# Eight more chunks solved in blocks of 32, early parts dealt later, and three inputs loaded in runs of eight steps

## The chip, the cores and the metric

The kernel runs on one core of a Trainium2 chip. The metric is the time of one execution in microseconds on the device; the median of three runs is given beside the lowest and the highest. The profile is taken from one more execution. In it, PE is the matrix engine and PEld its weight loads, DVE the vector engine, ACT the scalar engine, POOL the GpSimd engine, and SP an engine that here only issues DMAs.

## The reference

Two stages. The first is a recurrence over 768 steps for 4 batches x 8 heads with a state of 40 x 40 each; the second is a feed-forward network with a squared ReLU on its output.

```python
for t in range(S):                       # S = 768, D = 40
    y[:, :, t] = einsum('bhd,bhde->bhe', rt, state)
    Sa = einsum('bhde,bhe->bhd', state, at)
    state = state * wt[:, :, None, :] - einsum('bhd,bhe->bhde', Sa, bt) + einsum('bhd,bhe->bhde', vt, kt)
x = y.transpose(0, 2, 1, 3).reshape(B * S, H * D)     # 3072 x 320
h = maximum(x @ w_in, 0)                 # 320 x 2048
out = (h * h) @ w_out                    # 2048 x 320
```

The inputs of the recurrence are float32, laid out as batch, head, step, d. The weights w_in and w_out come as float64; the kernel reads their words and makes float32 of them.

## The kernel before

**Chunks.** The recurrence is done in 24 chunks of 128 steps, six for each batch; `order` (line 136) goes over the batches first, so chunks 0 to 3 are the first ones of the four batches. Within a chunk the steps depend on each other through a triangular system; its inverse is a matrix per head. A chunk has four parts:

- `early` (line 341) needs only w, a and b. It turns them so that d lies on the partitions (`turn`, line 311: four transposes on PE into one PSUM tile), makes running products of w in both directions with scans on DVE (lines 351, 352), reciprocals (355, 356), scales b and a (359, 360), and multiplies them to the triangular matrix N, which ACT copies out of PSUM (367 to 372). The pieces of N and the scaled rows are stored to DRAM (`kept_e`, `kept_q`, `kept_d`, `kept_m`, `kept_n`), because they are made several chunks ahead.
- `solve` (417, `solving` 420) inverts the triangular blocks on POOL, one column per step and two instructions per column (443, 445). It takes a whole unit of one, two or four chunks at once: `take` (406) reads their blocks from DRAM into `half_n`, and line 448 writes the inverse to `kept_t`. Units below `FINE` (line 299) are solved in blocks of `Q` = 32 steps, which is 31 columns; the others in blocks of `HC` = 64, which is 63 columns, with rows up to twice as long.
- `rest` (502) loads k, r, v, turns them, makes the masked products A and RV, and fetches the inverse (`inverses`, 452). For a unit of blocks of 64 the inverse comes straight into the tile `T`. For blocks of 32 it comes into `blocks`, and two blocks are joined into one of 64: a transpose on DVE (477), copies on ACT (479), 16 products on PE (487), a copy (489), 16 more products (494), a copy (496). `soon` (500) says whether the fetch is issued early in `rest`.
- `chain` (569) is the sequential part: eleven steps from PE to ACT or DVE and back, which use the state, T and N, and end in the tokens of the chunk.

**FFN.** `ffn` (663) works on groups of three chunks: eight steps with the first weight matrix, ReLU on ACT (679), squares on DVE (661), then twelve steps with the second. A group is 20 steps, all groups 160. It can start when three chunks are done and the first ten of 26 weight pieces are made. `rounding` (249) makes these pieces from the raw words, five DVE and two ACT instructions each; the raw words are staged in `w_out` and in `hidden`, whose last four tiles hold the small tiles of `spare` (337).

**Order.** After a prologue written out by hand (750 to 792), iteration i runs `chain(i)`, a share of FFN steps, one or two `prepare` (an `early`, with the loads of the next one), `rest(i + 1)` and some weight pieces. `weave` (707) deals their generator steps over twelve slots and emits the instructions in that order, which is the order of each engine's queue; what a generator has left after the twelve slots is run at the end, one generator after the other. `rest` gets nine steps in slots 2 to 11. `ahead` (796) says which early parts iteration i makes, `by_then` (802) how many FFN steps are done after it, `pieces_in` (806) how many weight pieces. After each iteration every unit whose chunks are all made is solved. One unit, number 4, is solved in two halves with an iteration between them (`AHEAD`, 810).

**Loads.** `fetch` (139) puts a chunk of an input into a ring tile `[128 steps, 8 heads, 64]`, of which 40 are data and 24 are a pad that a memset fills once. A load so has 1024 pieces of 40 words, 160 B each. All loads and most stores are issued by SP, in one queue.

Line 87 is the helper through which nearly all products go, line 314 the transposes of `turn`, line 108 all stores.

Of the kernel before, what the change touches and what calls it, by code (L numbers as in the profile page):

```python
# [12 lines left out]
Act = mybir.ActivationFunctionType  # L13
# [4 lines left out]
def kernel(  # L18
# [22 lines left out]
    nc = tc.nc  # L41
    ctx.enter_context(tc.manual_schedule())
    B, H, S, D = r.shape
# [45 lines left out]
    def single(name, shape):  # L89
        return const.tile(shape, FP32, tag=name, name=name)  # L90
# [25 lines left out]
    class Ring:  # L116
        def __init__(self, name, n, shape, fill, pads):
            self.tiles = [single(f"{name}{i}", shape) for i in range(n)]
            self.at = -1
            for t_ in self.tiles:  # L120
                nc.gpsimd.memset(pads(t_), fill)
# [4 lines left out]

    pads = lambda t_: t_[:, :, D:]
    rings = {}
    for nm, n, fill in (("w", 2, 1.0), ("ab", 4, 0.0)):
        rings[nm] = Ring(f"in_{nm}", n, [128, H, DP], fill, pads)  # L130

    def more_rings():
        for nm in ("k", "b", "r", "v"):
            rings[nm] = Ring(f"in_{nm}", 1 if nm == "r" else 2, [128, H, DP], 0.0, pads)

    order = [(bb, c) for c in range(NCH) for bb in range(B)]
    loaded, early_loaded = {}, {}

    def fetch(ring, src, i):
        bb, c = order[i]  # L140
        t_ = rings[ring].next()
        nc.sync.dma_start(out=t_[:, :, :D], in_=src[bb, :, c * C:(c + 1) * C, :].rearrange("h t d -> t h d"))
        return t_
# [27 lines left out]

    which = single("which", [128, 2])
    nc.gpsimd.memset(which, 0.0)
    for n in range(4):
        nc.gpsimd.memset(which[n * 32:(n + 1) * 32, n % 2:n % 2 + 1], 1.0)

# [118 lines left out]

    sizes = [1, 1] + [2] * 4 + [4] * ((len(order) - 12) // 4) + [2]
    units = [(sum(sizes[:u]), n) for u, n in enumerate(sizes)]

    FINE = 4
    SMALL = units[FINE][0]  # L300
# [10 lines left out]
    def turn(x_):  # L311
        p_ = psum(ps_w)
        for q in range(NP):
            nc.tensor.transpose(p_[:, q * 128:(q + 1) * 128], pair(x_, q), ident)  # L314
        return quads(p_)

    def products(l_, r_):
# [18 lines left out]

    def spare(name, i):
        at = NF * GB * C - (("mv", "turned", "joins").index(name) * 2 + i % 2 + 1) * H * Q
        return free_words[:, at:at + H * Q].rearrange("p (h t) -> p h t", h=H)

    def early(i, g=None):
# [5 lines left out]
        up, down, aT = (dec[:, n] for n in (UP, DOWN, A_))  # L347
        wT = turn(x_["w"])
        yield
# [3 lines left out]
        yield  # L353
        bT_, aT_ = turn(x_["b"]), turn(x_["a"])
        nc.vector.reciprocal(down[:, :, MID + 1:C + 1], up[:, :, MID + 1:C + 1])  # L355
# [30 lines left out]
        if g is None:  # L386
            store(kept_n[i], t_[:HC, :, HC:], 1)
        else:
            g["dec"], g["N"] = dec, new("N21", [HC, H, HC], 2)
            nc.scalar.copy(g["N"], t_[:HC, :, HC:])  # L390
            g["joins"] = spare("joins", i)
            for half in range(2):
                nc.scalar.copy(g["joins"][half * HC:half * HC + Q], joins(half))
# [8 lines left out]


    EARLIER = Q * HC

    def take(u, queues, words=slice(None)):
        first, nb = units[u]
        if u < FINE:
            kept = kept_q[first:first + nb].rearrange("b h f k s t -> (b h f k) (s t)")
        else:  # L410
            kept = kept_d[u].rearrange("b h f w -> (b h f) w")
        cols = classes(u)
        rows = 128 // cols
        for col in range(cols):
            queues[col % len(queues)].dma_start(out=part_of(u)[col * rows:(col + 1) * rows, words], in_=kept[:, words])  # L415

    def solve(u, between={}):
        run(solving(u, between))

    def solving(u, between={}, stop=None):  # L420

        first, nb = units[u]
        fine = u < FINE
        size = Q if fine else HC
        cols = classes(u)
        rows = 128 // cols
        part = part_of(u)
        words = size // cols * size
        at = u * Q * Q // 2 if fine else 0
        ts = solved[:, at:at + words]  # L430
        nc.gpsimd.memset(ts, 0.0)
        for col in range(cols):
            nc.gpsimd.memset(ts[col * rows:(col + 1) * rows, col::size + cols], -1.0)
        t3 = ts.rearrange("p (j t) -> p j t", t=size)
        for s in range(size - 1):
            if s in between:
                between[s]()
            if s == stop:
                yield
            n, m_ = s // cols + 1, size - 1 - s  # L440
            at = s * size + s + 1 if s < Q else Q * HC + (s - Q) * (Q + 1) + 1
            p_ = new("half_p", [128, 528], 1)[:, :n * m_].rearrange("p (j t) -> p j t", j=n)
            nc.gpsimd.tensor_tensor(p_, part[:, at:at + m_].unsqueeze(1).to_broadcast([128, n, m_]),  # L443
                                    t3[:, :n, s:s + 1].to_broadcast([128, n, m_]), Alu.mult)
            nc.gpsimd.tensor_tensor(t3[:, :n, s + 1:], t3[:, :n, s + 1:], p_, Alu.subtract)  # L445
        to = kept_t[u]
        to = to.rearrange("n b h f k j t -> (n b h f k) (j t)") if fine else to.rearrange("n b h f j t -> (n b h f) (j t)")
        nc.gpsimd.dma_start(out=to, in_=ts)
# [3 lines left out]
    def inverses(i, g, queue=nc.sync):  # L452
# [13 lines left out]
        if "N" not in g:  # L466
            g["N"] = new("N21", [HC, H, HC], 2)
            queue.dma_start(out=g["N"], in_=kept_n[i])
            if u < FINE:
                g["joins"] = spare("joins", i)  # L470
                for half in range(2):
                    queue.dma_start(out=g["joins"][half * HC:half * HC + Q], in_=kept_m[i][half])
        if u >= FINE:
            return
        yield
        upper_ = spare("turned", i)
        nc.vector.transpose(upper_.rearrange("p h t -> p (h t)"), blocks.rearrange("p h t -> p (h t)"))
        for n in range(2):
            nc.scalar.activation(T[:, :, n * Q:(n + 1) * Q], blocks, Act.Copy, scale=which[:, n:n + 1])
        yield  # L480
        small = lambda: psum(ps_w)[:, :H * Q].rearrange("p (h t) -> p h t", h=H)
        p_ = small()
        mv = spare("mv", i)
        ends_ = [(slice(half * HC, half * HC + Q), slice(half * HC + Q, (half + 1) * HC)) for half in range(2)]
        for h in range(H):
# [16 lines left out]
    def rest(i, g):  # L502
# [19 lines left out]
        while "v" not in x_:  # L522
            line.pop(0)[1]()
        nc.scalar.copy(rT, turn(x_["r"]))  # L524
        vT = turned("kvT", 1)
# [137 lines left out]
    def ffn():  # L663
        for gi in range(len(order) // GB):
# [3 lines left out]
            hid = []  # L668
            for f in range(0, NF, 2):
                square(hid[-2:])  # L670
                ps = [psum(ps_f if gi < len(order) // GB - 1 else ps_w)[:, :GB * C] for _ in range(2)]
                for e, p_ in enumerate(ps):
# [12 lines left out]
            for n in range(GB):  # L685
                bb, c = order[gi * GB + n]
                p_ = psum(ps_f if gi < len(order) // GB - 1 else ps_w)[:, :DM]
                for f in range(NF):
                    mm(p_, hid[f][:, n * C:(n + 1) * C], w_out[:, f], f == 0)
                    if f % PART == PART - 1 and f < NF - 1:  # L690
                        yield True
# [11 lines left out]
    def run(gen):  # L703
        for _ in gen:
            tick()
# [89 lines left out]
    TOTAL = 12  # L795
    ahead = {0: (4, 5), 1: (6, 7), 2: (8, 9), 3: (10,), 4: (11,), 5: (12, 13)}
    ahead.update({i: (i + 8,) for i in range(6, 9)})
    ahead[9] = (17, 18)
    ahead.update({i: (i + 9,) for i in range(10, len(order) - 9)})

    PER, LAG = NF // 2 + 4 * GB, 3
    by_then = [0] * B + [5]
    for i in range(B + 1, len(order)):
        by_then.append(min(by_then[-1] + 7, PER * (i + 1) // GB - PER - LAG if i > 2 * B else PER * i))
    share = {i: (n - (by_then[i - 1] if i else 0), 4 if i == B else 0) for i, n in enumerate(by_then)}
    pieces_in = {0: (4, TOTAL), 1: (6, TOTAL), 2: (6, TOTAL), 3: (7, TOTAL), B: (4, 4)}
    done = set(range(B))
    unit = unit_of[B]

    AHEAD, under_way = (FINE,), []  # L810
    for i in range(len(order)):
# [19 lines left out]
        while unit < len(units) and all(m_ in done for m_ in range(len(order)) if unit_of[m_] == unit):  # L831
            flush()
            if under_way:

                take(unit, own, slice(0, EARLIER))
                run(under_way.pop())
                take(unit, own, slice(EARLIER, Q * (HC + Q)))
            else:
                take(unit, own)
            if unit in AHEAD:  # L840
                under_way.append(solving(unit, stop=Q + 1))
                next(under_way[0])
            else:
                solve(unit)
            unit += 1
# [32 lines left out]
```

## Time and profile before

| | |
|---|---|
| median of three runs | 1046.84 us (1044.67 to 1049.31) |
| profiled execution, its own time | 1047.3 us |
| its span, first to last instruction | 1045.6 us |
| mean granted clock of PE | 0.915 |
| PE busy | 927.4 us, 89% of the span |
| PEld busy | 672.1 us, 64% |
| POOL busy | 670.6 us, 64% |
| DVE busy | 496.8 us, 48% |
| ACT busy | 273.0 us, 26% |
| DMA packets | 260360, of these 243724 under 512 B |
| DMA moved | 106.92 MB, 102 GB/s on average |

Busy time is the union of an engine's instructions; a granted clock below 1 says that PE ran at half rate for a part of the time. The start of line 583 marks the first step of each chunk's `chain`: 29.3, 105.4, 154.9, 204.9, 241.0 and 288.9 us for chunks 0 to 5, 479.6 for chunk 10, 645.5 for chunk 14 and 957.1 for chunk 23. The first FFN step's ReLU (679) starts at 252.8 us. POOL writes an inverse back (448) at 49.0, 76.3, 107.9 and 148.0 us for the four units in blocks of 32, at 251.4 and 338.8 for two chunks each in blocks of 64, at 475.1, 609.8 and 747.9 for four chunks each, and at 844.2 for the last two.

### The profile page before, as it was taken

Reading aid. Unit: us, or ns where it says so; the run is one execution under the profiler, and the core shown is the slowest. Engines: PE = TensorE matmul, PEld = TensorE weight load, DVE = VectorE, ACT = ScalarE, POOL = GpSimd, SP = SyncE. Lnnn points to the kernel's source line nnn. Section 1 sums busy time; section 2 is a strip of 40 time slices with the busy share of each in tenths; the row PEclk is TensorE's granted clock in tenths of the full one; section 3 lists DMA queues with packets and bytes.
Section 4 is the critical chain, followed back from the end, with each engine's and each line's share of the span. In section 5 each row is a group of like instructions: output and inputs, shape, how many; then the busy total and the mean of one; then the engine's idle time right before and its main releaser. Section 6 shows DMA issues by size and latency. Waiting matters only on the chain.

```text
span 1045.6 us, 19803 instructions
## 1 busy us (share of the span) xinstructions
PE 927.4 (89%) x7824; PEld 672.1 (64%) x7824; DVE 496.8 (48%) x940; ACT 273.0 (26%) x627; POOL 670.6 (64%) x1128
## 2 busy tenths in 40 slices
PE   6364665688999999997999999999999999999998
PEld 5253455576667766775677766775677567756656
DVE  5556685796554465453744545534432432222120
ACT  3132332334332133122232132113212311232020
POOL 4778454897898599995999949999668820000000
PEclk8656676667999999998999999999999999999999
DMA  8987989688184938198564596064425432520000
GB/s 108 154 145 146 178 196 179 163 158 147 43 137 92 193 55 136 24 164 194 61 113 90 87 183 119 21 118 59 115 50 98 66 72 49 98 30 7 23 0 19
DMA packets 260360, 106.92 MB, mean 102 GB/s; under 512 B 243724, under 2 KB 249356, under 8 KB 258604
## 3 DMA queue, kind: packets, MB, share of 16 engines
q1 hardware_dynamic: 255740, 86.65, 47.8%
q0 software_dynamic: 3440, 18.88, 7.8%
q8 instruction: 62, 1.02, 0.4%
q10 hardware_dynamic: 1088, 0.13, 0.1%
q14 instruction: 30, 0.25, 0.1%
HBM read 72.47 MB, written 31.19 MB: 99 GB/s over the span
## 4 chain that ended last, share of the span: by engine, by line
PE 52%; POOL 28%; DMA 10%; issue 5%; DVE 2%; ACT 2%; SPq 1%; POOLq 0%; DVEq 0%; ACTq 0%
PE ps_f L87 26%; POOL half_t L445 14%; POOL half_p L443 13%; PE ps_w L87 11%; PE ps_c L87 10%; DMA half_n<-kept_d 3%; PE ps_w L314 2%; DMA kept_t<-half_t 1%; DMA half_n<-kept_q 1%; DMA in_w<-in_w_dram 1%; DMA T<-kept_t 1%; DMA w_out<-in_moe_w_in_dram 1%; PE ps_w L542 1%; DMA kept_m<-N 1%; POOL half_n L415 1%
## 5 line engine op out<-in xcount | busy, mean ns | idle before, releaser
L443 POOL TENSOR_TENSOR half_p<-half_n,half_t 128x70 f32<-128x70 f32 (+52 forms) x502 | 298.9, 595 | 90.2 <-DMA half_n<-kept_d 39.8
L445 POOL TENSOR_TENSOR half_t<-half_t,half_p 128x70 f32<-128x70 f32 (+52 forms) x502 | 322.4, 642 | 39.3
L87 PE MATMUL ps_f<-w_out,hid 128*128 128x320 f32 x672 | 198.6, 440 | 0.0
L87 PE MATMUL ps_f<-tokens,w_in 128*128 128x384 f32 x448 | 162.3, 506 | 0.0
L661 DVE TENSOR_TENSOR hid<-hid 128x384 f32<-128x384 f32 x128 | 94.4, 752 | 139.4 <-ACT hid L679 139.0
L87 PEld LDWEIGHTS ps_f<-w_out,hid 128*128 128x128 f32 x672 | 121.6, 190 | 44.9 <-issue 2.1
L87 PEld LDWEIGHTS ps_f<-tokens,w_in 128*128 128x128 f32 x448 | 82.1, 193 | 77.2 <-issue 33.8
L679 ACT ACTIVATE hid<-ps_f 128x384 f32<-128x384 f32 x112 | 54.9, 490 | 201.1 <-PE ps_f L87 201.1
L330 DVE TENSOR_TENSOR A<-ps_w,upper 128x512 f32<-128x512 f32 x48 | 30.9, 686 | 108.0 <-PE ps_w L87 108.0
L87 PE MATMUL ps_w<-decay,bT 40*128 40x128 f32 x352 | 31.7, 330 | 33.2 <-DVE decay L360 29.5
L514 DVE TENSOR_TENSOR kvT<-ps_w,dec 128x512 f32<-128x512 f32 x24 | 16.5, 687 | 88.7 <-DMA dec<-kept_e 46.6
L87 PE MATMUL ps_f<-tokens,w_third 64*128 64x384 f32 x224 | 55.4, 540 | 0.0
L87 PEld LDWEIGHTS ps_w<-decay,bT 40*128 40x128 f32 x352 | 26.9, 229 | 41.8 <-DVE decay L360 26.7
L87 PE MATMUL ps_c<-xr,T 64*64 64x40 f32 x768 | 39.1, 242 | 13.7 <-ACT xr L592 6.7
L351 DVE TENSOR_TENSOR_SCAN decay<-ps_w,ones 128x64 f32<-128x64 f32 x88 | 23.8, 270 | 54.2 <-PE ps_w L314 54.1
L87 PEld LDWEIGHTS ps_c<-xr,T 64*64 64x64 f32 x768 | 32.5, 148 | 25.1 <-ACT xr L592 13.1
L330 DVE TENSOR_TENSOR RX<-ps_w,upper 128x512 f32<-128x512 f32 x48 | 30.8, 683 | 26.2 <-PE ps_w L87 25.9
L330 DVE TENSOR_TENSOR RV<-ps_w,upper 128x512 f32<-128x512 f32 x48 | 30.9, 686 | 18.1 <-PE ps_w L87 17.9
L355 DVE RECIPROCAL decay<-decay 128x256 f32<-128x256 f32 x22 | 38.3, 1739 | 0.0
L356 DVE RECIPROCAL decay<-decay 128x256 f32<-128x256 f32 x22 | 37.3, 1694 | 0.0
L87 PE MATMUL ps_w<-rT,xnT 40*128 40x128 f32 x384 | 34.2, 293 | 2.4 <-ACT rT L524 2.4
L524 ACT COPY rT<-ps_w 128x512 f32<-128x512 f32 x24 | 14.0, 585 | 82.5 <-PE ps_w L314 82.5
(139 smaller groups left out, 1391.0 us busy)
## 6 DMA issues: line engine op xcount, KB each, us to landing
kept_e<-decay SPq DMA_DIRECT2D x22, 633.8 KB
dec<-kept_e SPq DMA_DIRECT2D x22, 633.8 KB
hid<-in_moe_w_out_dram SPq DMA_DIRECT2D x16, 320.0 KB
half_n<-kept_d POOLq DMA_DIRECT2D x6, 768.0 KB, 11.4
in_w<-in_w_dram SPq DMA_DIRECT2D x24, 160.0 KB
in_ab<-in_b_dram SPq DMA_DIRECT2D x24, 160.0 KB
in_ab<-in_a_dram SPq DMA_DIRECT2D x24, 160.0 KB
in_k<-in_k_dram SPq DMA_DIRECT2D x24, 160.0 KB
```

The source lines that it names most:

```text
L87: nc.tensor.matmul(o, l_, r_, start=start, stop=True, skip_group_check=True)
L314: nc.tensor.transpose(p_[:, q * 128:(q + 1) * 128], pair(x_, q), ident)
L330: nc.vector.tensor_tensor(t_, p_, over4(upper), Alu.mult)
L351: nc.vector.tensor_tensor_scan(up[:, q, MID + 1:C + 1], wT[:, q, MID:], ones, 1.0, Alu.mult, Alu.mult)
L355: nc.vector.reciprocal(down[:, :, MID + 1:C + 1], up[:, :, MID + 1:C + 1])
L356: nc.vector.reciprocal(up[:, :, :MID], down[:, :, :MID])
L443: nc.gpsimd.tensor_tensor(p_, part[:, at:at + m_].unsqueeze(1).to_broadcast([128, n, m_]), t3[:, :n, s:s + 1].to_broadcast([128, n, m_]), ...
L445: nc.gpsimd.tensor_tensor(t3[:, :n, s + 1:], t3[:, :n, s + 1:], p_, Alu.subtract)
L514: nc.vector.tensor_tensor(kT, kT_, down[:, :, 1:C + 1], Alu.mult)
L524: nc.scalar.copy(rT, turn(x_["r"]))
L661: nc.vector.tensor_tensor(h_, h_, h_, Alu.mult)
L679: nc.scalar.activation(h_, p_, Act.Relu)
```

## The change

- `FINE` goes from 4 to 8 and `sizes` from units of 1, 1, 2, 2, 2, 2, 4, 4, 4, 2 chunks to 1, 1, 2, 2, 2, 2, 2, 2, 4, 4, 2. So chunks 6 to 13 are solved in blocks of 32, in units of two, and are joined in `rest`. The solve in two halves goes.
- `ahead` deals the early parts later: one each in iterations 1 to 4, two each in 5 to 8. The FFN share begins in iteration 3 with two steps, and is two ahead up to chunk 14; the weight pieces are dealt a little earlier to match.
- The joins of chunks from 2 on use the still empty half of `T` and one tile `turned_blocks` in place of tiles in `hidden`. The first FFN group starts with the four tiles of `hidden` that stage no weights, and takes PSUM from `ps_w` while weight pieces are left.
- w, a and r of chunks 0 to 9 are loaded in runs: partition (run n, head h) gets eight steps of one head, 320 words in one piece. `turn_runs` turns such a tile with 16 products: for each of the eight steps and each parity of the head, the tile's 64 columns are the weights and the 64 identity columns of that parity are streamed. When a ring tile goes back to the old layout, its pads are filled then, on DVE.

```diff
+    PACKED, RUN = 10, 8
+    unpadded = set()
+    flat = lambda t_: t_.rearrange("t h d -> t (h d)")
...
+    def in_runs(i, src):
+        return i < PACKED and any(src is x_ for x_ in (w, a, r))
     def fetch(ring, src, i):
         bb, c = order[i]
         t_ = rings[ring].next()
+        if in_runs(i, src):
+            nc.sync.dma_start(out=flat(t_)[:, :RUN * D],
+                              in_=src[bb, :, c * C:(c + 1) * C, :].rearrange("h (n t) d -> n h (t d)", t=RUN))
+            return t_
+        if id(t_) in unpadded:
+            unpadded.discard(id(t_))
+            nc.vector.memset(pads(t_), 1.0 if ring == "w" else 0.0)
         nc.sync.dma_start(out=t_[:, :, :D], in_=src[bb, :, c * C:(c + 1) * C, :].rearrange("h t d -> t h d"))
...
-    sizes = [1, 1] + [2] * 4 + [4] * ((len(order) - 12) // 4) + [2]
+    sizes = [1, 1] + [2] * 6 + [4] * ((len(order) - 16) // 4) + [2]
-    FINE = 4
+    FINE = 8
...
+    def turn_runs(x_):
+        p_ = quads(psum(ps_w))
+        x_ = flat(x_)
+        by_head_ = ident.rearrange("p (n q e) -> p q e n", q=NP, e=2)
+        for t in range(RUN):
+            for e in range(2):
+                o = p_[e * DP:(e + 1) * DP].rearrange("p q (n t) -> p q n t", t=RUN)[:, :, :, t]
+                nc.tensor.matmul(o, x_[:, t * D:t * D + DP], by_head_[:, :, e], start=True, stop=True, skip_group_check=True)
+        return p_
...
-        wT = turn(x_["w"])
+        turn_ = turn_runs if i < PACKED else turn
+        wT = turn_(x_["w"])
...
-        bT_, aT_ = turn(x_["b"]), turn(x_["a"])
+        bT_, aT_ = turn(x_["b"]), turn_(x_["a"])
...
-                g["joins"] = spare("joins", i)
+                g["joins"] = T[:, :, Q:]
...
-        upper_ = spare("turned", i)
+        upper_ = mv = turned_blocks
         nc.vector.transpose(upper_.rearrange("p h t -> p (h t)"), blocks.rearrange("p h t -> p (h t)"))
-        for n in range(2):
-            nc.scalar.activation(T[:, :, n * Q:(n + 1) * Q], blocks, Act.Copy, scale=which[:, n:n + 1])
+        nc.scalar.activation(T[:, :, :Q], blocks, Act.Copy, scale=which)
+        for _, two in ends_:
+            nc.scalar.copy(T[two, :, Q:], blocks[two])
...
-        nc.scalar.copy(rT, turn(x_["r"]))
+        nc.scalar.copy(rT, (turn_runs if i < PACKED else turn)(x_["r"]))
...
-            for f in range(0, NF, 2):
+            for f in range(-4 if gi == 0 else 0, NF - 4 if gi == 0 else NF, 2):
+                f %= NF
-                ps = [psum(ps_f if gi < len(order) // GB - 1 else ps_w)[:, :GB * C] for _ in range(2)]
+                ps = [psum(ps_w if left() or gi == len(order) // GB - 1 else ps_f)[:, :GB * C] for _ in range(2)]
...
-    ahead = {0: (4, 5), 1: (6, 7), 2: (8, 9), 3: (10,), 4: (11,), 5: (12, 13)}
-    ahead.update({i: (i + 8,) for i in range(6, 9)})
-    ahead[9] = (17, 18)
-    ahead.update({i: (i + 9,) for i in range(10, len(order) - 9)})
+    ahead = {0: (4, 5), 1: (6,), 2: (7,), 3: (8,), 4: (9,), 5: (10, 11), 6: (12, 13), 7: (14, 15), 8: (16, 17)}
+    ahead.update({i: (i + 9,) for i in range(9, len(order) - 9)})
-    by_then = [0] * B + [5]
+    by_then = [0] * (B - 1) + [2, 7]
-    share = {i: (n - (by_then[i - 1] if i else 0), 4 if i == B else 0) for i, n in enumerate(by_then)}
-    pieces_in = {0: (4, TOTAL), 1: (6, TOTAL), 2: (6, TOTAL), 3: (7, TOTAL), B: (4, 4)}
+    share = {i: (n - (by_then[i - 1] if i else 0), {B - 1: 9, B: 4}.get(i, 0)) for i, n in enumerate(by_then)}
+    pieces_in = {0: (4, TOTAL), 1: (6, TOTAL), 2: (7, TOTAL), 3: (6, 9), B: (4, 4)}
```

## The prediction

> **What bounds the kernel now.** I read the page first, for which engine is full when; then the busy time in stretches cut at the iterations; then the waits of the early stretch; then single rows for prices.
>
> From the page, the slices of 26.1 us:
>
> ```profile
> PE   6364665688999999997999999999999999999998
> POOL 4778454897898599995999949999668820000000
> PEclk8656676667999999998999999999999999999999
> DMA  8987989688184938198564596064425432520000
> ```
>
> There are two stages. Up to slice 9 (about 250 us) PE is half idle at a low granted clock, while DMA is full. From there to the end PE is full at full clock. POOL looks full for 800 us and the chain of waits passes through it, but PE has FFN products to do meanwhile: past 250 us POOL makes PE idle once, in slice 18.
>
> The cuts below are the starts of line 583 (first step of `chain`) in iterations 1 to 5. Columns: stretch, its length, then PE, PEld, DVE, ACT and POOL busy (count), granted clock, DMA share, GB/s.
>
> ```profile
> 105.40:154.90 49.50, 30.25 (x321) 25.18 (x320) 37.99 (x70) 17.07 (x39) 27.05 (x76) 0.67 0.96 185
> 154.90:204.90 50.00, 31.16 (x320) 26.89 (x320) 32.58 (x71) 15.38 (x39) 31.56 (x64) 0.64 0.86 169
> 204.90:241.00 36.10, 29.54 (x312) 25.54 (x312) 31.37 (x68) 15.09 (x36) 32.40 (x53) 0.65 0.84 162
> 241.00:288.90 47.90, 43.93 (x382) 30.30 (x384) 27.51 (x55) 15.71 (x38) 39.23 (x84) 0.86 0.52 93
> 288.90:329.20 40.30, 39.78 (x353) 29.01 (x354) 24.77 (x47) 11.64 (x28) 35.99 (x56) 1.00 0.59 97
> ```
>
> Iterations 1 and 2, with two early parts each, take 50 us; iteration 3, with one, takes 36 and keeps DVE 87% busy. DVE paces these three, with DMA waits on top. From iteration 4 PE paces everything, so each us that PE gains or loses there is a us of the end.
>
> The DMA waits, for iteration 2 (waits) and for line 142 (count: ns least/median/most):
>
> ```profile
> PE ps_w L314 <- DMA in_w<-in_w_dram: 7.9, 1, 7.9
> L142 SPq DMA_DIRECT2D in_w<-in_w_dram x24: 394/840/8417, 0.8 to 609.8; - x24
> ```
>
> SP normally issues a load in 0.4 to 0.8 us, but one held it for 8.4 us: a queue full of short packets.
>
> **The early parts.** Chunk 7 moves from iteration 1 to 2, chunks 8 and 9 from 2 to 3 and 4, 10 and 11 to 5, 12 and 13 to 6; from 9 on nothing is left moved. One early part costs DVE 8 scans x 0.27 + 1.74 + 1.69 + 0.66 + 0.68 = 6.9 us, ACT 1.7 us of copies, PE three turns and 16 instructions, and SP three loads and at least six stores. Iterations 1 and 2 lose one each and then look like iteration 3, so I price them by it. A weight piece costs DVE 3.42 us at 512 columns (five instructions of lines 264 to 275) and 2.43 at 320. Iteration 1 has six wide pieces where iteration 3 had seven narrow: 36.1 + 20.5 - 17.0 = 39.6. Iteration 2, with seven narrow, 36.1. Iteration 3 drops a piece (-2.4) and gets two FFN steps at its end, 3.64 us each at full clock (12 instructions in the chain of waits) and some 5.5 at 0.65, less 4 that PE's idle time takes: 36.1 - 2.4 + 7 = 40.7. Sum 116.4 against 135.6: **-19.2**. Bounds: -9 (only DVE's two early parts less the FFN steps) to -33 (iterations 1 and 2 fall to DVE's own busy time less 6.9).
>
> Later this is paid for. Two early parts (chunks 9 and 10) now fall in the full PE stage: turns 0.60 + 1.09, products 1.16, 2.85 each, **+5.7**. The two FFN steps leave it: **-7.3**. The FFN quota is the same again from chunk 15 on. The steps that now run before the weights are done take PSUM from `ps_w`, which the early parts and `rest` use too; DVE's pace in iteration 3 covers a wait there, and without that it is a us or two.
>
> **Loads in runs.** A load was 1024 packets of 160 B, 23.6 ns each before 250 us, on 16 engines 1.5 us; in runs it is 128 packets of 1280 B, which elsewhere in this trace take 55 to 70 ns, 0.5 us. Some 25 of the 30 loads fall before 250 us: 25 us less transfer. Waits on DMA of PE and ACT in iterations 0 to 3 are near 30 us (in_w 7.9 and 3.3, in_k 4.9, blocks 7.2, 5.1 and 4.5), partly parallel, the 7.9 already gone in my template. I take **-11**, bounds 0 and -20.
>
> **Turns by products.** 4 transposes (0.60 us at full clock) become 16 products of 64 columns in two instructions each, 32 in all. The trace has no such form. Nearest: 128*64 with 40 columns, 0.64 us for 16, so 1.3 per turn; with 128 columns, 1.09, so 2.2. Closer to the first: 1.4, or +0.8 per turn (bounds +0.7 and +1.6; whether a stride in the moving operand costs more no row shows). Iteration 4 on has seven (a, w of chunk 9, r of 5 to 9): **+5.6**, up to 11. At half clock it is +1.1; the other 23 lie under DVE or POOL, except the first two and about half of those in iterations 0 to 3: **+7**. Without that cover they cost 25. The memsets of pads from chunk 10 on are five on DVE, 0.26 us each by POOL's row of that shape, under PE: nothing.
>
> The Trainium skill, TensorE: Matmul & The Clock Gate, section Terms, has a transpose mode four times faster for FP32, and TensorEngine Tiling (Array Packing), section Restrictions, says that column tiling, which these 64-column outputs use, turns it off. This trace shows a factor of two (a 128-column product in two instructions of 145 ns, a transpose in one of 150); by the page's factor a turn would be 2.4 us and the seven would cost 12.6.
>
> **Blocks of 32 for chunks 6 to 13.** POOL gets cheaper: 87 to 94 us for two chunks and 136 for four become 31 to 38 for two. What it frees on the path is one stall:
>
> ```profile
> 489.53 1.08 PE L87 MATMUL ps_c<-xr,T 64*64 64x40 f32 x16 [5.44 <-DMA T<-kept_t]
> ```
>
> 5.44 us, and then 6.8 us at half clock, 3.4 more: **-8.8**. In exchange each of the eight chunks must be joined: DVE transpose, ACT copies, 32 instructions on PE, a copy, 32 more. `rest` has more steps than the nine that are woven, so its last ones run at the end of the iteration with nothing between. The one such case in the full stage, chunk 5:
>
> ```profile
> 281.83 0.69 PE L87 MATMUL ps_w<-hid 32*32 32x32 f32 x32
> ...
> 284.13 1.08 PE L87 MATMUL ps_w<-blocks,hid 32*32 32x32 f32 x32 [1.60 <-ACT hid L489]
> ...
> 285.14 1.98 PE L87 MATMUL ps_c<-A,in_v 128*64 128x128 f32 x16
> ```
>
> PE waits 1.60 us for the copy, which stands in ACT's queue behind the early part's copies; behind the waiting product on PE are the next chunk's products and all FFN. The stretch from 285.1 to 288.4 then has a granted clock of 0.50, so the next products took 1.98 where 1.09 is usual: three groups there took 0.39, 0.89 and 0.67 us more than usual, 1.95 us lost. Per chunk 0.69 + 0.69 + 1.6 = 3.0, eight: **+23.8**. The clock loss I count half the time, since a gap split over two windows of 3.4 us costs none: **+7.8**. Chunks 8, 10 and 12 fetch their blocks later and leave both joins to the unwoven end: **+3** (1 each, by the 2.43 us gap at 101.8). Bounds for the joins: 11 (gaps filled) and 42 (the clock lost each time). ACT and DVE have room (28.7 and 15.5 of 40.3 us idle in iteration 5). SP gets two stores and two loads more per chunk, about 2.3 us, under PE.
>
> For the clock the same skill page, in "What's actually happening", wants a whole idle window of about 3.4 us; here 1.6 us in one window was enough. By the page the sum would be 7.8 lower.
>
> **Sum**: -19.2 - 11 + 7 + 5.7 - 7.3 + 5.6 - 8.8 + 23.8 + 7.8 + 3 = **+6.6**. Made against the profiled execution (span 1045.6, time 1047.3); the median of the three runs is 1046.84, half a us below that time. Forecast 1053.4, say 1053.
>
> **Rivals.**
> 1. Faster: the short packets set the pace of iterations 0 to 3 more than DVE does. For: DMA share 0.84 to 0.96 there, SP held 8.4 us. Against: DVE 87% busy in iteration 3 with DMA just as full. Price: the early gain at its bound, -33, with transfers at -20: +6.6 - 13.8 - 9 = -16.2, so 1031. It decides once iterations 0 to 3 together win 30 us.
> 2. No change: the unwoven joins meet no clock loss and ACT is free in time (gap 1 us): -7.8 - 4.8, +6.6 becomes -6; with half of that, 1047.
> 3. Slower still: POOL late for chunks 14 to 17, whose solve now starts after iteration 8 (about 420 us) and takes 136. It would end near 560; chunk 14 reads it near 600. Past that point it costs the lateness and half as much again in clock; 20 us late is 1083.
> 4. The parts do less than they say: the strided products take twice as long, which eats the early gain too: +7 and +5.6 double, 1066.
>
> **Chances.** Forecast 0.42 (slower 0.35, same 0.07), rival 1 0.33 (faster 0.31, same 0.02), rival 2 0.14 (same 0.11, faster 0.02, slower 0.01), rivals 3 and 4 together 0.11 (slower). Faster 0.33, same 0.20, slower 0.47, with 0.5% (5.2 us) as what a measurement of this kernel can tell. Own range of the forecast 1045 to 1062; to hold 8 in 10 it reaches to rival 1's middle and rival 4: 1027 to 1068.
>
> **What would show it.** Right: iterations 1 and 2 near 40 and 36 us; FFN's first step (line 679) near 212 us in place of 252.8; no T wait of 5 us; waits of PE on line 489 eight times more, with half clock behind several; PE busy up by 20 us or more past iteration 4. Wrong: iteration 4 starting before 205 us (rival 1); no half clock past iteration 4 (rival 2); a long wait on T at chunk 14 or 18 (rival 3); turns over 2.5 us at full clock (rival 4).

## The result and the profile after

The changed kernel takes 1088.72 us (median of 4 runs, 1084.46 to 1090.30) against 1048.07 for the kernel before on the same chip: ratio 1.0379, 95% interval 1.0328 to 1.0430, slower. The sign of the forecast was right; the size, 1053, was not, and the time lies outside the range. Ratios here and below leave disturbed runs out, so a median of all runs can differ a little from what its ratio says.

The profiled execution has a span of 1088.4 us, 42.8 above the one of before. Its slices, now of 27.2 us:

```profile
PE   7486778689998998988999899999999999999998
...
POOL 4788530530273571029999204999858830000000
PEclk8776656689899998998989899999999999999999
DMA  6768982742748675493542827537074413430000
```

PE is a little fuller early, but from slice 12 on it has five 8s where it had 9s and one 7, and the granted clock is at 8 in slices 10, 15, 18, 20 and 22, three of them the same. POOL has holes of two slices: it waits for its data, and nothing waits for it. Next the stretches by iteration, cut as before at the first step of `chain` (line 611 now), iterations 1 to 5; columns as before.

```profile
103.80:146.10 42.30, 30.36 (x376) 25.48 (x376) 32.18 (x58) 16.10 (x35) 27.46 (x79) 0.66 0.85 170
146.10:183.80 37.70, 31.97 (x376) 27.05 (x376) 28.91 (x63) 15.16 (x38) 0.61 (x1) 0.64 0.59 131
183.80:236.50 52.70, 38.41 (x420) 29.25 (x420) 30.26 (x66) 16.82 (x39) 25.30 (x68) 0.73 0.57 120
236.50:286.90 50.40, 47.41 (x466) 33.74 (x466) 26.35 (x60) 16.38 (x38) 1.81 (x5) 0.87 0.44 70
286.90:330.50 43.60, 41.00 (x437) 31.22 (x437) 21.14 (x44) 12.60 (x30) 23.05 (x63) 0.98 0.66 123
```

Iterations 1 and 2 fell from 49.5 and 50.0 to 42.3 and 37.7. Iteration 3 rose from 36.1 to 52.7 and took most of it back. The rest was lost in iterations 5 to 13, where PE sets the pace. They are one row each, of before and then of after:

```profile
288.90:645.50 356.60, 347.41 (x2973) 248.31 (x2974) 186.74 (x339) 92.94 (x216) 295.38 (x375) 0.99 0.64 117
```

```profile
286.90:691.60 404.70, 379.99 (x3645) 276.36 (x3646) 192.44 (x368) 117.05 (x275) 215.22 (x371) 0.96 0.59 106
```

PE has 672 instructions more, a lower clock and more idle time. With the prediction's terms put into the same stretches (its -7.3 for FFN steps named no place and stands in the last row), the account is:

```
stretch                forecast  measured  missed by
up to iteration 3        -27.8     -21.1      6.7
iteration 3               +4.6     +16.6     12.0
iteration 4               +5.2      +2.5     -2.7
iterations 5 to 13       +31.9     +48.1     16.2
from 14 on, FFN steps     -7.3      -3.3      4.0
sum                       +6.6     +42.8     36.2
```

Of the 24 FFN products that iteration 3 takes over, 16 are missing from iteration 14 on and 8 in iterations 5 to 13 (603 in place of 611), so some 2.4 of the -7.3 belongs to the row of iterations 5 to 13, which misses by 18.6 then.

So two places ask for experiments: iteration 3, and iterations 5 to 13.

### The profile page after: what moved, and what is told of

Same layout as the page of the kernel before. It is cut to its first block, busy times and chain, and to the rows that moved or that the text cites. A ratio compares the mean times of both kernels' runs of the same rounds, so it can differ in the third digit from the quotient of the medians.

```text
span 1088.4 us, 22511 instructions
## 1 busy us (share of the span) xinstructions
PE 982.1 (90%) x9176; PEld 717.7 (66%) x9176; DVE 487.5 (45%) x953; ACT 299.3 (28%) x689; POOL 508.1 (47%) x990
## 4 chain that ended last, share of the span: by engine, by line
PE 76%; DMA 9%; ACT 5%; issue 3%; SPq 3%; DVE 3%; POOL 3%; DVEq 0%; ACTq 0%; POOLq 0%
PE ps_f L87 34%; PE ps_w L87 16%; PE ps_c L87 16%; PE ps_w L336 4%; PE ps_w L346 3%; DMA dec<-kept_e 2%; DMA blocks<-kept_t 2%; DMA in_v<-in_v_dram 1%; DMA in_w<-in_w_dram 1%; POOL half_t L472 1%; POOL half_p L470 1%; ACT turned_blocks L517 1%; PE ps_w L570 1%; PE ps_c L616 1%; PE ps_c L645 1%
## 5 line engine op out<-in xcount | busy, mean ns | idle before, releaser
L470 POOL TENSOR_TENSOR half_p<-half_n,half_t 128x126 f32<-128x126 f32 (+44 forms) x437 | 222.3, 509 | 106.3 <-DMA half_n<-kept_q 40.0
L472 POOL TENSOR_TENSOR half_t<-half_t,half_p 128x126 f32<-128x126 f32 (+44 forms) x437 | 241.3, 552 | 34.2
L87 PE MATMUL ps_f<-w_out,hid 128*128 128x320 f32 x672 | 203.5, 448 | 0.0
L87 PE MATMUL ps_f<-tokens,w_in 128*128 128x384 f32 x432 | 155.4, 503 | 0.0
L689 DVE TENSOR_TENSOR hid<-hid 128x384 f32<-128x384 f32 x128 | 85.0, 682 | 123.2 <-ACT hid L709 123.0
L87 PEld LDWEIGHTS ps_f<-tokens,w_in 128*128 128x128 f32 x432 | 78.6, 192 | 74.4 <-issue 32.0
L448 POOL DMA_DIRECT2D half_n<-kept_q x18 | 9.4, 527 | 124.4 <-DMA kept_q<-N 78.8
L448 POOL DMA_DIRECT2D half_n<-kept_d x8 | 4.0, 506 | 100.4 <-DMA kept_d<-N 100.3
L87 PEld LDWEIGHTS ps_c<-xr,T 64*64 64x64 f32 x768 | 32.3, 148 | 18.6 <-ACT xr L620 11.9
L87 PE MATMUL ps_w<-blocks,turned_blocks 32*32 32x32 f32 x448 | 16.8, 222 | 28.4 <-ACT turned_blocks L517 26.8
L87 PE MATMUL ps_w<-decay,bT 40*128 40x128 f32 x352 | 26.6, 291 | 13.2 <-DVE decay L396 10.2
```

What stands on the lines that cost most here:

```text
L87: nc.tensor.matmul(o, l_, r_, start=start, stop=True, skip_group_check=True)
L689: nc.vector.tensor_tensor(h_, h_, h_, Alu.mult)
```

## Experiments

Each is a change of the changed kernel unless the kernel before is named. The median in us and the ratio to the kernel before (with its 95% interval) follow each expectation. `...` in a code cut stands for text left out.

**The joins of chunks 6 to 13.** In iterations 5 to 13 the waits of PE (in all, times, longest) are, and one join looks like this (start, duration):

```profile
PE ps_w L87 <- ACT turned_blocks L517: 17.4, 8, 3.0
PE ps_c L87 <- ACT xr L620: 2.1, 4, 0.5
PE ps_w L336 <- DMA in_w<-in_w_dram: 1.5, 1, 1.5
```

```profile
420.06 0.69 PE L87 MATMUL ps_w<-turned_blocks,T 32*32 32x32 f32 x32
423.76 1.45 PE L87 MATMUL ps_w<-blocks,turned_blocks 32*32 32x32 f32 x32 [3.00 <-ACT turned_blocks L517]
425.13 1.98 PE L87 MATMUL ps_c<-A,in_v 128*64 128x128 f32 x16
```

The second product of the join waits 3.0 us for ACT's copy of the first, and then it and its successor run at half clock. What the joins are worth in all, the first run shows, which leaves them out, and with them two steps of `rest`:

```
         yield
+        if i >= B + 2:
+            return
         small = lambda: psum(ps_w)[:, :H * Q].rearrange(...)
```

> The changed kernel without the two join products and their copies for chunks 6 to 13 (that part of the inverse is left out; fetch, transpose on DVE and the copies on ACT stay). Theory: a join costs PE 1.4 us of its own, 1.6 to 3.0 us of waiting for ACT's copy and, most times, a window at half clock; from iteration 5 to 13 idle time grew by 15.7 us over before and half clock by 14.6 us of work, and 8 x 1.4 = 11 us are the products: without them about 40 us less, 1049 (1043 to 1056). Rival: most of these 48 us are the early parts that moved there, the turns and fetches that come late; then it stays over 1065.

1055.92 us, ratio 1.0065 (1.0030 to 1.0099). The joins cost 33 us: 8 x 1.38 of products, 12.4 of idle time, and 9.5 of clock (half of 36.0 against 17.0 us at half clock in iterations 5 to 13), together 32.9 by the profiles. But without them the kernel is still not faster than before. In iterations 5 to 13 its row and its longest waits are:

```profile
284.00:656.10 372.10, 359.85 (x3133) 260.03 (x3134) 190.05 (x368) 105.58 (x243) 212.78 (x371) 0.98 0.64 116
```

```profile
PE ps_w L336 <- DMA in_k<-in_k_dram: 4.4, 2, 3.5
PE ps_w L336 <- DMA in_w<-in_w_dram: 2.8, 1, 2.8
```

15.5 us more than before, where the prediction without its terms for the joins has 2.7 less (31.9 - 34.6): 18.2 us of this stretch were missed, and not by the joins. There is no wait on T; PE waits for loads in its place, 8.7 us in all.

Can the gaps be filled?

```
-        jobs.append((some(second, n), n, begin, TOTAL))
+        late = 2 if B + 2 <= i + 1 < SMALL else 0
+        jobs.append((some(second, n - late), n - late, begin, TOTAL))
+        if late:
+            jobs.append((some(second, late), late, TOTAL, TOTAL + 2))
...
-            jobs.append((rest(i + 1, ready[i + 1]), 9, 2, TOTAL))
+            jobs.append((rest(i + 1, ready[i + 1]), 11, 3, TOTAL + 2) if late else (rest(...), 9, 2, TOTAL))
```

> The changed kernel, with two more slots in the iterations that prepare chunks 6 to 13, and the last steps of rest and two FFN steps dealt into them, so that an FFN step stands between the two join products. Theory: in the changed kernel PE waits 17.4 us in eight gaps of 1.6 to 3.0 us in front of the second join product, and is granted half clock for some 36 us from iteration 5 to 12, which is 18 us of work; with FFN between, the gaps fall under 0.6 us and half clock is rare, so 1088.7 falls by 25 to 32 to about 1060. Rival: what the joins cost is their own instructions and the early parts that moved; then the time stays at 1083 to 1090.

1080.64, ratio 1.0306 (1.0255 to 1.0356): 8 us in place of 28. The eight waits are gone, but the gaps have moved, as the longest waits of PE in iterations 5 to 13 show:

```profile
PE ps_c L645 <- ACT minus_x L632: 5.5, 8, 0.7
PE ps_c L87 <- ACT minus_x L631: 3.1, 8, 0.4
PE ps_c L616 <- ACT xnT L611: 3.0, 5, 0.7
```

The FFN steps were covering copies of the chain before; taken from there, they leave 0.7 us holes there. PE's idle time in iterations 5 to 12 went only from 24.5 to 17.9 us. The same cover can be spent only once.

**Iteration 3.** The chain begins at 183.8, before at 204.9. SP's issues around it, before and after (start, time that SP took, DMAs):

```profile
190.36 6.32 SPq L108 DMA_DIRECT2D tokens<-tokens  x8
...
200.27 1.82 SPq L108 DMA_DIRECT2D kept_d<-N  x4
...
203.54 0.40 SPq L142 DMA_DIRECT2D in_k<-in_k_dram  x1
```

```profile
175.35 6.78 SPq L108 DMA_DIRECT2D tokens<-tokens  x8
...
183.26 3.31 SPq L108 DMA_DIRECT2D kept_q<-N  x2
186.63 0.66 SPq L108 DMA_DIRECT2D kept_m<-N  x1
187.33 1.76 SPq L108 DMA_DIRECT2D kept_q<-N  x2
...
191.17 0.40 SPq L164 DMA_DIRECT2D in_k<-in_k_dram  x1
191.62 0.57 SPq L174 DMA_DIRECT2D dec<-kept_e  x1
```

`in_k` is issued 7.4 us after the chain's start, behind the first group's token stores and chunk 7's block stores, where before it went out 1.4 us ahead of it. The block stores just ahead of it took SP 1.8 us before (four `kept_d`) and 6.3 us now (four `kept_q`, two `kept_m`). PE and DVE wait in this iteration:

```profile
PE ps_w L336 <- DMA in_k<-in_k_dram: 6.6, 1, 6.6
```

```profile
DVE kvT L542 <- DMA dec<-kept_e: 9.0, 1, 9.0
```

First attempt: all block stores of chunks 6 to 13 to POOL's queue.

```
-  store(kept..., nc.scalar if g is not None and n else nc.sync)
+  store(kept..., nc.scalar if g is not None and n else nc.gpsimd if B + 2 <= i < SMALL else nc.sync)
-  store(kept_m[i][half], joins(half), 1)
+  store(kept_m[i][half], joins(half), 1, nc.gpsimd if i >= B + 2 else nc.sync)
```

> The changed kernel, with the stores of the 32-blocks of chunks 6 to 13 (kept_q, kept_m) issued by POOL, not SP. Theory: iteration 3 takes 52.7 us, not the 40.7 forecast, because SP has eight token stores and seven stores of N ahead of the next loads, so in_k is issued 7.4 us after the chain's first step where it was 1.4 us ahead of it before; with six stores off SP the 6.6 us wait for in_k shrinks to under 2 and iteration 3 to about 44 us, the whole to about 1080. Rival: the DMA engines are full and the order of issue does not matter; then iteration 3 stays over 50 us and the whole at 1085 to 1091.

1099.19, ratio 1.0478 (1.0419 to 1.0537), 10 us slower than the changed kernel. The token stores still stood ahead of `in_k`, which went out 3.5 us after the chain's start in place of 7.4; PE waited 7.6 us for it all the same, so the time of issue alone does not explain the wait. And later chunks' stores stood behind POOL's solve: N was ready at 309.4, its stores went out at 331.9, ACT then waited 11.9 us to write the next N, and the longest wait of PE for the copy of a join grew from 3.0 to 10.9 us. Second attempt: of the block stores only chunk 7's, and the token stores as well.

```
-  store(t_[row:row + m_, j], t_[at:at + m_, h // 2], 1)
+  store(t_[row:row + m_, j], t_[at:at + m_, h // 2], 1, nc.gpsimd if i < GB else nc.sync)
```

> The changed kernel with the eight token stores of the first group and the 32-block stores of chunk 7, all at the end of iteration 2, issued by POOL, which is idle there, in place of SP. Theory: iteration 3 waits 6.6 us for in_k and 9 us for dec because SP issues these loads only 7 to 8 us after the iteration has begun, and with 14 fewer stores ahead they are issued at its start: iteration 3 goes from 52.7 to 44 to 46, the whole to about 1081. Rival: the loads take 6 us to land behind packets of other transfers whoever issues them; moving six of the stores to POOL had left iteration 3 at 53.9: then it stays over 50 us.

1078.63, ratio 1.0304 (1.0261 to 1.0347): 10 us, as expected. Iteration 3 takes 44.1 us, and the longest waits of PE in it are:

```profile
PE ps_w L87 <- ACT turned_blocks L517: 1.6, 1, 1.6
PE ps_c L616 <- ACT xnT L611: 1.0, 1, 1.0
```

The wait for `in_k` is gone; it was issued at 182.75, 1.5 us ahead of the chain. Which of the two kinds of stores counts more, no run separates. The FFN steps were the rival for this stretch:

```
-    by_then = [0] * (B - 1) + [2, 7]
+    by_then = [0] * B + [5]
-    pieces_in = {..., 3: (6, 9), B: (4, 4)}
+    pieces_in = {..., 3: (6, TOTAL), B: (4, 4)}
```

> The changed kernel with FFN starting in iteration 4 as before (5 steps), none in iteration 3, whose weight pieces go over all twelve slots. Theory: of the 16.6 us by which iteration 3 is longer than before, about 7 are the two FFN steps and the rest loads that come late: iteration 3 goes from 52.7 to about 45 us and the whole stays within 4 us of 1088.7, for the steps are done later. Rival: the FFN steps take PSUM that the early part and rest wait for, and cost more than themselves: then iteration 3 falls under 40 us and the whole by over 6 us.

1091.42, ratio 1.0434 (1.0384 to 1.0484). Iteration 3 is 5.3 us shorter (47.4), and the time is not: the steps come back later. Their place is worth nothing here.

**Loads in runs and turns by products.** Without them (`PACKED = 0`), and alone on the kernel before:

> The changed kernel with w, a, r of all chunks loaded as before and turned by transposes. Theory: a turn by products takes 2.08 us at any clock where 1.4 was forecast and a transpose takes 0.60, so runs cost some 10 us from iteration 4 on and 8 before it, against 11 us of DMA waits that they save; without them about 1082 (1075 to 1092). Rival: the runs are what made iterations 1 and 2 fast; without them these go back towards 50 us and the whole goes over 1098.

1084.67, ratio 1.0345 (1.0285 to 1.0406). Iteration 4 starts 3.2 us later than with them, and what they gain there is lost from then on.

> The kernel before, with only the runs and their turns added. Theory: 8 us of turns before iteration 4 and five turns after it (1.5 us each, 7.5) against 11 us of DMA waits saved: about 1052 (1045 to 1060). Rival: short packets set the pace of iterations 0 to 3; then these lose 20 us or more and the whole is about 1030.

1048.33, ratio 0.9991 (0.9961 to 1.0021), the same. In its profile iteration 4 starts at 237.5 in place of 241.0: load relief less turns is 3.5, where the prediction had 11 - 7 = 4. From there on iterations 5 to 8 take 8.8 us longer, and iteration 10 takes 7.0 less (43.9 in place of 50.9): the wait of 5.44 us on T is gone here too, with the solve left as it was.

The turn itself was mis-sized. Two turns of after, one at half clock and one at full:

```profile
185.44 2.14 PE L346 MATMUL ps_w<-ident,in_w 128*64 128x64 f32 x32
...
447.05 2.08 PE L346 MATMUL ps_w<-ident,in_r 128*64 128x64 f32 x32
```

It takes nearly the same time at either clock, so the granted clock does not set it. The identity columns that a product streams lie 32 bytes apart. One run made them adjacent, which leaves the turned rows in another order:

```
-  by_head_ = ident.rearrange("p (n q e) -> p q e n", q=NP, e=2)
+  by_head_ = ident.rearrange("p (e q n) -> p q e n", q=NP, e=2)
```

> The changed kernel with the turns' moving operand, 64 columns of the identity, taken side by side in place of every eighth pair (which sorts the turned rows wrongly; the same instructions otherwise). Theory: a turn takes 2.08 us at either clock because the moving columns are 32 B apart; side by side it takes 1.3 to 1.5 us at full clock. Rival: it is the stride in PSUM of the output, or the weight loads; then it stays at 2.0 to 2.15.

A turn took 1.13 us at full clock and 1.98 at half; its one execution took 1076.52 us. The output's stride in PSUM and the weight loads, the rival, were as before. A second layout reads four runs of 16 adjacent columns and keeps the order of the turned rows, since the loads put the heads first:

```
-  in_=src[bb, :, c * C:(c + 1) * C, :].rearrange("h (n t) d -> n h (t d)", t=RUN)
+  in_=src[bb, :, c * C:(c + 1) * C, :].rearrange("h (n t) d -> h n (t d)", t=RUN)
-  by_head_ = ident.rearrange("p (n q e) -> p q e n", q=NP, e=2)
+  by_head_ = ident.rearrange("p (q e n) -> p q e n", q=NP, e=2)
```

> The changed kernel with the runs of w, a and r laid out by head first, so that the identity columns that a turn's product reads are four runs of 16 adjacent ones in place of 64 columns 32 bytes apart; the output is the reference's. Theory (the stride of the moving operand sets the 2.08 us of a turn at either clock): turns of 1.1 to 1.2 us at full clock and still about 2.0 at half clock, time 1074 to 1079. Rival (the gain of the run with sorted rows was chance or came from elsewhere): turns stay at 2.1 or the time stays at 1085 or more.

1082.54, ratio 1.0308 (1.0266 to 1.0350). The same two turns:

```profile
186.92 1.98 PE L346 MATMUL ps_w<-ident,in_w 128*64 128x64 f32 x32
...
444.12 1.13 PE L346 MATMUL ps_w<-ident,in_r 128*64 128x64 f32 x32
```

The duration is the theory's; the gain is 6 us and not 12, with intervals that just overlap. It is about that of the seven late turns, 7 x 0.95 = 6.7 at most; that other engines cover the early ones fits, and was not shown. The 12 of the single run did not come back in four.

> The kernel before with the loads in runs laid out by head first, blocks and dealing as before. Its form with strided columns was at 1048.3. Theory (some 15 to 18 turns there stood at full clock at 2.08 us, and each us of PE from iteration 4 on is a us of the end): 1036 to 1042, faster than the kernel before. Rival (in iterations 0 to 3 other engines cover the turns, and only the six late ones count, 0.95 us each): 1042 to 1044. If runs and turns still bring nothing: 1048.

1046.22, ratio 0.9988 (0.9954 to 1.0022): no difference that can be told.

**All repairs, and fewer joins.** The three repairs together, and then with `FINE = 7`:

> The changed kernel with three repairs at once: runs laid out by head first, two FFN steps between the last steps of a join, and the first group's token stores issued by POOL. If the three losses are separate, 1088.7 - 12 - 8 - 10 = 1059, iteration 3 at 43 to 45 us. If they overlap, 1064 to 1070. In either case still slower than before, since the joins' own products and copies remain.

1068.95, ratio 1.0169 (1.0117 to 1.0222). With 6 for the turns the sum would be 1065; iteration 3 took 44.7, and iterations 0 to 2 ended 3.0 us later than in the profile of after. Iteration 0 differs by up to 6 us between profiles (73.4 to 79.4), so single profiles don't add up closer than this.

> The same three repairs, and chunks 12 and 13 in one block of 64 steps again, as before the change, so that six chunks are joined in place of eight. The joins cost some 33 us for eight, so 4 each: 8 us less than with eight, 1051 if the repairs add up. Rival (POOL, which then works some 90 us on these two chunks, is late for chunk 12 or 14 and PE waits for T): gain under 3 us, with a wait on T of several us near 500 or 600 us.

1066.28, ratio 1.0164 (1.0120 to 1.0208): 2.7 less, within the scatter, and the rival's gain (under 3) more than the theory's (8). Iteration 11 lost its join (34.0 in place of 40.2), but PE waited 1.85 us for T and, in iteration 7, 4.3 us for `in_w`. Inconclusive between theory and rival.

**Is that the whole loss?** The joins left out, the other two terms repaired:

> The changed kernel without the two join products and their copies for chunks 6 to 13 (so their T lacks the coupling between the halves of a block), with the runs laid out by head first and the first group's token stores issued by POOL. Without the joins alone it stood at 1055.9, not faster than before. Theory (joins, late loads in iteration 3 and slow turns are the whole loss, and they are separate): 1055.9 - 9 - 6 = 1041, which is 7 faster than before. Rival (another loss is left, or the repairs overlap as in the run of all three repairs, which came out 10 above its sum): 1047 to 1052, no gain over before.

1047.31, ratio 0.9956 (0.9920 to 0.9993). By the ratio some 5 us faster than before, by the medians of all runs 0.9 (1048.21): the rival's case, 1047 to 1052. The three terms account for the slowdown, but the gain that was to be there without them is not, so a loss is left. In its profile, one of its longer runs (1049.8), iteration 5 starts 11.6 us earlier than before (277.3), and from there to iteration 14 18.5 are lost. SP and PE in iteration 6:

```profile
314.80 3.05 SPq L108 DMA_DIRECT2D kept_q<-N  x2
317.90 1.00 SPq L108 DMA_DIRECT2D kept_m<-N  x1
319.00 1.03 SPq L108 DMA_DIRECT2D kept_q<-N  x2
...
324.83 2.34 SPq L164 DMA_DIRECT2D in_b<-in_b_dram  x1
327.22 5.79 SPq L164 DMA_DIRECT2D in_w<-in_w_dram  x1
```

```profile
337.07 1.09 PE L336 MATMUL ps_w<-ident,in_w 128*128 128x128 f32 x4 [4.36 <-DMA in_w<-in_w_dram]
```

Seven stores, then loads of which one holds SP for 5.8 us, then PE idle for 4.4. In iteration 9 PE waits another 1.5 us for `in_k` and 4.35 for DVE, which waited 15.0 us for the load of `dec`. To tell the stores from the loads, the stores of chunks 8 to 13 went to ACT, without and with the joins:

```
-  nc.gpsimd if i == B + 3 else nc.sync
+  nc.gpsimd if i == B + 3 else nc.scalar if B + 3 < i < SMALL else nc.sync
```

> As the run without joins and with both terms repaired (so T lacks the coupling between the halves for chunks 6 to 13), and the six block stores of each of chunks 8 to 13 issued by ACT in place of SP. There SP issued seven stores of two new blocks in 7.5 us just ahead of the loads of iteration 6, in_b and in_w held it 2.3 and 5.8 us more, and PE waited 1.3 and 4.4 us for in_k and in_w, with 14 us at half clock behind it. Theory (SP's extra stores make the late loads late): these waits shrink under 1 us and iteration 6 falls from 50 to about 41; 1047.3 - 8 = 1039, iterations 5 to 13 at 365 to 368 in place of 375. Rival (the short packets of in_b and in_w hold SP whatever stands ahead): iteration 6 stays at 46 or more, 1045 to 1049. If ACT's copies are held up by its stores instead: 1050 or more.

1046.62, ratio 0.9981 (0.9957 to 1.0004). Iterations 5 to 13 take 368.0 us, as the theory said (365 to 368). But the time is the rival's (1045 to 1049, where the theory had 1039), and iteration 6 takes 45.9 us, the rival's 46 and not 41; iteration 5 starts 7.5 us later than in the profile above, at 284.8. The waits moved:

```profile
PE ps_w L87 <- ACT kvT L556: 3.4, 1, 3.4
PE ps_w L336 <- DMA in_k<-in_k_dram: 3.1, 1, 3.1
PE ps_c L618 <- ACT xnT L613: 2.4, 1, 2.4
```

In iteration 6 the wait for `in_w` falls from 4.4 to 0.7 us and the one for `in_k` from 1.3 to none, and a copy of ACT comes 3.4 us late instead: ACT had waited 10.1 us behind its own stores. The wait for `in_k` that stays is that of iteration 9. It stands behind four `kept_d` stores of chunk 17, which this edit leaves on SP (452.81 to 456.38); before, `in_k` of that iteration was issued at 442.30, ahead of such stores.

> All of the computation: the changed kernel with the three repairs (head first, FFN steps between the last steps of a join, the first group's token stores by POOL) and the block stores of chunks 8 to 13 issued by ACT. The run with the three repairs alone stood at 1069. Theory (SP's extra stores make late loads late): 1061. Rival (they are covered by the joins' own gaps): 1069. If ACT is held up: 1072 or more.

1077.06, ratio 1.0258 (1.0217 to 1.0298), 8 slower than without that edit. ACT is held up: in iteration 6 it waits 10.9 us behind its stores, and PE 5.8 us for its copy (348.93). No complete version among these is faster than the kernel before by more than can be told.

## Why the prediction missed

**Right.** The direction, and its main reason. The joins were put at 23.8 + 7.8 + 3 = 34.6 and cost 33; their gaps have the forecast sizes (1.6 to 1.9 us, 3.0 for chunks 8, 10 and 12). That the sum is so close is in part luck: 15.8 us of idle time were counted and 12.4 went, 7.8 of clock were counted and 9.5 went. Iterations 1 and 2 came within 3 us of 39.6 and 36.1. The net of runs and early turns, -4, was -3.5. Past iteration 4 PE waits for an inverse once, 0.73 us at 834.3 (rival 3 falls), and half clock does appear there (rival 2 falls). Rival 1 falls with the start of iteration 4 at 236.5; its bound of -33 does not follow from its own rows, which give 31.1 + 25.7 + 40.7 - 135.6 = -38. Rival 4's sign, a turn over 2.5 us, did not come, but its mechanism did: the stride makes a turn 2.08 where it takes 1.13 without. One sign of being right failed: the first FFN step's ReLU starts at 223.7 us and not near 212, as late as iteration 3 is.

**"36.1 - 2.4 + 7 = 40.7", iteration 3.** It was 52.7. The template had its loads issued ahead of the chain. I priced the iteration by the work of the engines and let SP's times stand as they were, though iterations 1 and 2 now end 21 us earlier, and the token stores and chunk 7's longer block stores fall just ahead of the loads. Taking those stores off SP gave back 8.6 of the 12.0 in the iteration and 10 of the total.

**"T stall removed, -8.8".** The wait on T did go, but the work that came forward met the next late thing, the loads. Without the joins, iterations 5 to 13 have 3.1 us more idle time and 5.1 us more clock loss than before, so the step is worth nothing like -8.8 but about +8.2: 17 us of the miss. With the joins in place the waits for loads come to 2.8 us in place of 8.7; most of them hide in the joins' gaps. "SP gets two stores and two loads more per chunk, about 2.3 us, under PE" is the sentence that failed: with two early parts in iterations 5 and 6 it is seven stores in 7.5 us ahead of the loads. Nor does SP "normally" issue a load in 0.4 to 0.8 us: before, the median for `in_b` was 3.9 us. How much of these waits the stores make, and how much the short packets of `in_b` and `in_w` behind them, stays open: off SP, the stores took 5.0 of 5.6 us of the waits of iteration 6 with them, but made ACT late, and those of iteration 9 were not moved.

**"Closer to the first: 1.4" for a turn.** It was 2.08, near the upper bound of 2.2, which I had named and dropped; the stride that "no row shows" was the reason. Seven late turns make +10.4 in place of +5.6, which is 4.8 of the miss. The factor of four for transposes in the Trainium skill, TensorE: Matmul & The Clock Gate, section Terms, would give 2.4, close to the number but not the cause: with adjacent columns the same turn takes 1.13, about twice a turn by transposes (0.60), near the factor of two that the prediction read from the trace before.

**"A gap split over two windows costs none", the clock, +7.8.** Four of the eight joins' gaps did cost clock, as counted, but each of these was followed by 6.8 us at half clock and not 3.4: 4 x 3.4 = 13.6 of lost work, where the work lost to half clock in these iterations fell by 9.5 without the joins. That it was four is luck: with the token stores on POOL, the same gaps were followed by half clock all eight times. What the Trainium skill, TensorE: Matmul & The Clock Gate, section "What's actually happening", asks for, a whole idle window, is again not needed: 3.0 and 1.6 us were enough.

Up to iteration 3, 6.7 us less came in than hoped. Iterations 1 and 2 and the load relief share that, and no run separates them.

## What to carry to other kernels

When a stage gets shorter, go through the DMA queue that feeds the next stage issue by issue: stores that used to fall in slack now stand ahead of its first load. A stall that is removed is won only up to the next thing that is late, so look up what lands just after it. Work that fills a gap has been filling another; count it once.

## What the runs showed of the hardware

In a turn by FP32 products whose moving columns lie 32 bytes apart, an instruction of 64 columns comes on average every 57 ns at full clock and every 60 at half; with runs of 16 or 64 adjacent columns it is 29 to 30 ns at full and 54 at half. At half clock the stride costs a tenth, at full clock it doubles the time.

A gap of 1.60 us on PE was followed by 3.4 us at half clock in the kernel before (285.1) and by 6.8 us for the same gap in the changed one (281.9); other gaps of 1.6 to 1.9 us (325.4, 369.9, 646.2) were followed by none. How long the clock stays down is set by more than the length of the gap.

Where a gap falls goes with it, too. In the changed kernel the half-clock stretches from this gap to the end of iteration 13 begin at 281.91 us and 41, 61, 68, 82 and 94 steps of 3.413 us later, and last two steps each. Of the joins' gaps, the four without half clock lie across two such steps with at most 1.08 us in either (0.86 and 1.08, 0.79 and 0.86, 0.92 and 0.73, 0.98 and 0.62); the other four have 1.24 to 2.96 us in one. So the prediction's gap that is split over two windows and costs nothing is there. The limit is not sharp: with the token stores on POOL, 1.07 us in one step was enough.
